# Three small early reads of q and of two weight matrices, added at the start of a fused attention and feed-forward kernel

## The chip, the cores and the metric

The kernel runs on one core of a Trainium2 chip. The metric is device time in microseconds (us) per execution. Executions agree within some tenths of a per cent (the six of the kernel before ran from 325.63 to 327.38 us). A ratio quoted below is the mean time of one kernel's fast runs over the mean of the other kernel's fast runs of the same rounds, so it is not quite the ratio of the medians that stand beside it. Some executions are slow, with a much lower mean granted clock; they are left out of every comparison of times.

Words used: TensorE is PE in the profile (PEld is its weight load), VectorE is DVE, ScalarE is ACT, GpSimd is POOL, SyncE is SP. On the page of the kernel before, the transfers issued by SP and ACT stand on hardware queues (q1 with 41.23 MB and q10 with 0.13 MB), those issued by GpSimd on its software queue (q0 with 11.80 MB). All times inside a profile count from the first instruction.

## The reference

```python
# q, k, v: (8, 8, 576, 64) float32
r = np.maximum(x, 0.0); phi(x) = concat([r * cos_w, r * sin_w], -1)   # cos, sin of pi/2 * pos / S
kv  = einsum('bhsf,bhsd->bhfd', phi(k), v);  z = sum(phi(k), axis=2)
att = einsum('bhsf,bhfd->bhsd', phi(q), kv) / (einsum('bhsf,bhf->bhs', phi(q), z) + 1e-6)
x   = att.transpose(0, 2, 1, 3).reshape(4608, 512)
out = (gelu(x @ w_gate) * (x @ w_val)) @ w_out                        # d_ff 1536
```

## The kernel before

The kernel treats a batch of q, k, v at a time. The three weight matrices are loaded once, cast to bf16 on the way. The first 20 us are a hand-placed start; after them TensorE works without a break in this profile.

```python
    consts = ctx.enter_context(tc.tile_pool(name="consts", bufs=1))     # pools lie one after another
    weights = ctx.enter_context(tc.tile_pool(name="weights", bufs=1))
    inp = ctx.enter_context(tc.tile_pool(name="inp", bufs=2))           # staging of k, q, v in float32
    ...
    load(nc.sync, "k", 0, 0, 2)              # 576 KB each, rows of 2,304 bytes
    load(nc.sync, "k", 0, 2, 4)
    load(nc.sync, "q", 0, 0, NP, 0, JA)      # 512 KB, rows of 1,024 bytes
    load(nc.sync, "v", 0, 0, 2)
    load(nc.sync, "v", 0, 2, 4)
    load(nc.sync, "q", 0, 0, NP, JA, R)      # 640 KB, rows of 1,280 bytes
    ...
        nc.gpsimd.memset(t[:, :, :, D:D + 1], 1.0)      # the two vx tiles
        vx_tiles.append(t)
    gate = consts.tile([128, 1], FP32)
    gate2 = consts.tile([128, 1], FP32)
    ...
    cast_v(0, 0, 2, dve_copy)
    nc.gpsimd.tensor_copy(gate, staged["v", 0][:, 0, 0:1])   # GpSimd waits for v's first half
    load_w(0, 2)                                             # first W group: w_gate, then w_val
    load_w(2, 2)
    nc.gpsimd.tensor_copy(gate2, wg_sb[:, 0, 0:1])           # waits for w_gate's first group
    load_w(4, 2)
    nc.gpsimd.tensor_copy(gate2, wv_sb[:, 0, 0:1])           # waits for w_val's first group
    ...
    dummies(22)                              # products of zeros, to keep TensorE busy at the start
```

The three `gate` copies hold the weights back until v's first half is there, so that W does not compete with v: in the profile before, the first copy starts at 9.39 us and the first W issue at 10.11. They are also good markers in a profile: there each starts when the tile it reads has landed (9.39, 14.29 and 16.57 us, each after a wait for a DMA).

Of the kernel before, what the change touches and what calls it, by code (L numbers as in the profile page):

```python
# [9 lines left out]
FP32 = mybir.dt.float32  # L10
# [6 lines left out]
def kernel(  # L17
# [13 lines left out]
    nc = tc.nc  # L31
# [17 lines left out]
    consts = ctx.enter_context(tc.tile_pool(name="consts", bufs=1))  # L49
# [21 lines left out]
    def rows(t, b):  # L71
        return t[b].rearrange("(m i) (p j) d -> (i p) m (j d)", i=2, j=R)
# [15 lines left out]
    wg_r = moe_w_gate.rearrange("(ct p) j -> p ct j", p=128)  # L88
    wv_r = moe_w_val.rearrange("(ct p) j -> p ct j", p=128)
# [41 lines left out]
    for i in range(2):  # L131
        t = consts.tile([128, NP, R, D + 1], BF16, name=f"vx{i}")
        nc.gpsimd.memset(t[:, :, :, D:D + 1], 1.0)
        vx_tiles.append(t)
    gate = consts.tile([128, 1], FP32)
    gate2 = consts.tile([128, 1], FP32)

# [470 lines left out]
    for n in range(1, NB):  # L608
# [4 lines left out]
        for jt in range(JT):  # L613
# [18 lines left out]
            if b < B:  # L632
# [12 lines left out]
                i = jt - t_nm - 1  # L645
# [8 lines left out]
                i = jt - 1 - n if n <= 2 else -1  # L654
                if 0 <= i < 3:
                    prep_third("k", b, i)
                i = 2 * (jt - 5) if n == 1 else jt - (4 if n == 2 else 0)
# [4 lines left out]
                i = jt - 9  # L662
# [73 lines left out]
```

## Time and profile before

The time before was 327.24 us (median of three runs, 326.32 to 327.38). The profile is of one more run, of 325.91 us.

| what | value | view |
|---|---|---|
| TensorE busy, whole span | 316.8 of 323.9 us | the page, busy times |
| TensorE busy, 20 us to 320 us | all of it | table of stretches |
| v's second half seen landed (its cast starts) | 10.76 us | chain of waits, timeline |
| w_gate's and w_val's first groups seen landed | 14.29 and 16.57 us | timeline, the gate copies |
| first 512-column product | 21.11 us | timeline |

The table of stretches of the kernel before. Columns: the stretch and its length, busy time and number of instructions of each engine, the granted TensorE clock as a share of full speed, the busy share of the DMA engines, GB/s.

```profile
15.00:20.00 5.00, 4.76 (x84) 4.11 (x82) 4.12 (x12) 3.66 (x8) 4.08 (x8) 1.00 1.36 173
20.00:25.00 5.00, 5.00 (x42) 2.88 (x40) 1.70 (x4) 2.86 (x7) 3.65 (x5) 1.00 1.42 192
60.00:320.00 260.00, 260.00 (x1870) 130.70 (x1867) 130.32 (x306) 116.81 (x242) 0.00 (x0) 1.00 0.54 139
```

TensorE is full from 20 us on. A change at the start can gain or lose only by the moment at which this unbroken work begins.

The chain of waits of the kernel before, first 30 us. Columns: start, length, what.

```profile
2.27 0.51 SPq L80
2.78 0.04 issue
2.82 7.92 DMA vf<-in_v_dram
10.74 0.02 issue
10.76 0.86 DVE vx L179
...
13.95 1.29 DVE x_sb L322 x2
...
16.64 0.89 PE ps L372 x16
...
19.49 1.79 PE ps L372 x32
21.27 6.91 PE ps L400 x32
```

The start waits for v's second half and then for VectorE's steps. No weight stands in the chain. The waits of TensorE in the same stretch (who waited for whom: us in total, times, longest) say the same: nothing here is a transfer.

```profile
PE ps L140 <- POOL dummy L113: 1.5, 1, 1.5
PE ps L204 <- ACT qp L160: 1.0, 2, 0.9
PE ps L218 <- DVE vx L179: 0.2, 1, 0.2
PE ps L357 <- DVE x_sb L295: 0.2, 1, 0.2
PE ps L218 <- POOL gate L458: 0.2, 1, 0.2
```

The timeline of the kernel before around the first weights (start, length, engine, line, operation, tiles; in brackets the idle time before it and what ended it):

```profile
14.29 0.18 POOL L461 CAST gate<-wg_sb 128x1 f32<-128x1 bf16 x1 [0.89 <-DMA wg_sb<-in_moe_w_gate_dram]
...
16.48 0.61 PE L372 MATMUL ps<-xT,wg_sb 128*128 128x128 bf16 x8
...
16.57 0.18 POOL L463 CAST gate<-wv_sb 128x1 f32<-128x1 bf16 x1 [0.66 <-DMA wv_sb<-in_moe_w_val_dram]
...
16.93 0.61 PE L372 MATMUL ps<-xT,wv_sb 128*128 128x128 bf16 x8
```

w_val's group lands 0.36 us before its first product starts.

The trace also records every packet of every transfer: start, queue, size and time taken. A 1,024-byte packet of q takes 46 ns, but a few packets at 5.5 to 5.9 us took 380 to 453 ns, soon after q's load begins (its first packet starts at 5.16 us); three at 12.15 us, soon after W begins (at 11.77 us, with 59 ns), took 376 to 414 ns. (W stands for the weights w_gate and w_val.)

### The profile page before, as it was taken

The page shows a single profiled execution, that of the slowest core. Times are in us where ns is not written, and L with a number is a line of the kernel's source. Part 1 is how long each engine was busy: PE and PEld are TensorE (multiplying, and loading weights), DVE is VectorE, ACT ScalarE, POOL GpSimd, SP SyncE. Part 2 cuts the span into 40 slices and gives each one's busy share as a digit, 9 for nine tenths or more (in the row PEclk, how much of TensorE's full clock was granted, in tenths as well). Part 3 has the DMA queues.
Part 4 walks back from the last instruction along what each step waited for, and adds up shares of the span by engine and source line. Part 5 has one row for each costly group of instructions (what it writes and reads, how often), then busy time and mean ns, then how long its engine had stood idle before and what let it go on. Part 6 is the DMA issues. An engine that isn't in the chain of part 4 may idle for free.

```text
span 323.9 us, 6340 instructions
## 1 busy us (share of the span) xinstructions
PE 316.8 (98%) x2451; PEld 164.5 (51%) x2451; DVE 170.3 (53%) x407; ACT 159.3 (49%) x336; POOL 26.0 (8%) x43
## 2 busy tenths in 40 slices
PE   8899999999999999999999999999999999999995
PEld 3574556555754564545544554445544444444443
DVE  5854677759665952793586348544532222222211
ACT  7864858946466832673457336633222332222220
POOL 6684410000000000000000000000000000000000
PEclk9999999999999999999999999999999999999999
DMA  7999999842999689938957990543431111111124
GB/s 274 249 186 273 297 352 366 230 111 51 323 216 354 166 147 383 201 83 251 330 96 157 383 232 1 137 102 78 85 73 33 34 32 32 35 32 32 34 65 98
DMA packets 69102, 53.57 MB, mean 165 GB/s; under 512 B 45392, under 2 KB 54352, under 8 KB 69072
## 3 DMA queue, kind: packets, MB, share of 16 engines
q1 hardware_dynamic: 59264, 41.23, 48.1%
q0 software_dynamic: 9648, 11.80, 15.7%
q8 instruction: 19, 0.31, 0.4%
q10 hardware_dynamic: 160, 0.13, 0.1%
q14 instruction: 11, 0.09, 0.1%
HBM read 37.75 MB, written 9.44 MB: 146 GB/s over the span
## 4 chain that ended last, share of the span: by engine, by line
PE 93%; DMA 2%; DVE 2%; SPq 1%; issue 0%; DVEq 0%
PE ps L400 57%; PE ps L430 28%; PE ps L282 3%; PE ps L241 3%; DMA vf<-in_v_dram 2%; PE ps L204 1%; PE ps L372 1%; PE ps L697 1%; SPq L80 1%; PE ps L357 0%; DVE qp L162 0%; DVE x_sb L322 0%; DVE vx L179 0%; DVE x_sb L295 0%; DVE qT L486 0%
## 5 line engine op out<-in xcount | busy, mean ns | idle before, releaser
L409 DVE TENSOR_TENSOR hT<-gel,ps 128x512 bf16<-128x512 f32 (+1 forms) x114 | 74.1, 650 | 128.9 <-PE ps L400 126.0
L408 ACT ACTIVATE gel<-ps 128x512 f32<-128x512 f32 (+1 forms) x114 | 64.8, 569 | 109.7 <-PE ps L400 108.0
L400 PE MATMUL ps<-xT,wv_sb 128*128 128x512 bf16 (+1 forms) x456 | 110.2, 364 | 0.0
L400 PE MATMUL ps<-xT,wg_sb 128*128 128x512 bf16 (+1 forms) x456 | 110.2, 364 | 0.0
L430 PE MATMUL ps<-wo_sb,hT 128*128 128x512 bf16 x420 | 105.8, 379 | 0.0
L400 PEld LDWEIGHTS <-wv_sb 128*128 128x128 bf16 x456 | 44.6, 98 | 47.0
L400 PEld LDWEIGHTS <-wg_sb 128*128 128x128 bf16 x456 | 44.0, 98 | 46.1
L430 PEld LDWEIGHTS <-hT 128*128 128x128 bf16 x420 | 38.3, 98 | 39.4
L439 ACT COPY o_sb<-ps 128x512 f32<-128x512 f32 x34 | 19.9, 587 | 29.9 <-PE ps L430 27.6
L160 ACT ACTIVATE qp<-qf,sin_t 128x256 bf16<-128x256 f32 x72 | 32.0, 501 | 0.4 <-DMA qf<-in_q_dram 0.4
L160 ACT ACTIVATE kp<-kf,sin_t 128x256 bf16<-128x256 f32 (+1 forms) x73 | 29.9, 479 | 0.9 <-DMA kf<-in_k_dram 0.9
L295 DVE TENSOR_TENSOR x_sb<-ps,rec 128x512 bf16<-128x512 f32 x38 | 26.3, 691 | 1.3
L162 DVE TENSOR_SCALAR qp<-qf,cos_t 128x256 bf16<-128x256 f32 x71 | 21.8, 353 | 2.3 <-DMA qf<-in_q_dram 2.3
L282 PEld LDWEIGHTS <-qT 128*128 128x128 bf16 x304 | 14.6, 98 | 7.9 <-ACT qT L486 0.3
L162 DVE TENSOR_SCALAR kp<-kf,cos_t 128x256 bf16<-128x256 f32 x63 | 18.3, 349 | 0.0
L282 PE MATMUL ps<-kv_sb,qT 128*128 128x65 bf16 x304 | 16.0, 194 | 0.0
L179 DVE CAST vx<-vf 128x1152 bf16<-128x1152 f32 (+1 forms) x15 | 12.0, 804 | 0.8 <-DMA vf<-in_v_dram 0.8
L250 ACT CAST kv_sb<-ps 128x260 bf16<-128x260 f32 x14 | 4.6, 383 | 12.9 <-PE ps L241 12.9
L241 PEld LDWEIGHTS <-kp 64*128 64x128 bf16 x504 | 8.5, 95 | 3.0 <-issue 3.0
L140 PE MATMUL ps<-dummy 128*128 128x512 bf16 x27 | 8.4, 457 | 1.5 <-POOL dummy L113 1.5
L241 PE MATMUL ps<-vx,kp 64*128 64x65 bf16 x504 | 9.3, 191 | 0.0
L294 DVE RECIPROCAL rec<-den 128x8 f32<-128x8 f32 x38 | 7.7, 203 | 1.3
(60 smaller groups left out, 100.6 us busy)
## 6 DMA issues: line engine op xcount, KB each, us to landing
out_dram<-o_sb SPq DMA_DIRECT2D x70, 128.0 KB, 2.6
kf<-in_k_dram SPq DMA_DIRECT2D x12, 576.0 KB, 6.2
vf<-in_v_dram SPq DMA_DIRECT2D x12, 576.0 KB, 8.3
qf<-in_q_dram SPq DMA_DIRECT2D x10, 576.0 KB, 5.0
qf<-in_q_dram POOLq DMA_DIRECT2D x4, 576.0 KB, 12.2
kf<-in_k_dram POOLq DMA_DIRECT2D x4, 576.0 KB, 12.5
vf<-in_v_dram POOLq DMA_DIRECT2D x4, 576.0 KB, 12.8
wg_sb<-in_moe_w_gate_dram POOLq DMA_DIRECT2D x6, 256.0 KB, 6.4
```

Source lines behind the costliest of these rows:

```text
L140: nc.tensor.matmul(bank(to), lhsT=dummy[:, 0:128], rhs=dummy, start=True, stop=True)
L160: nc.scalar.activation(o, i, AF.Relu, scale=tab[:, j:j + 1])
L162: (eng or nc.vector).tensor_scalar(o, i, 0.0, tab[:, j:j + 1], op0=ALU.max, op1=ALU.mult)
L179: copy(vx_tiles[b % 2][:, m0:m1, j0:j1, 0:D], staged["v", b][:, m0:m1, j0 * D:j1 * D].rearrange("p m (j d) -> p m j d", d=D),)
L241: nc.tensor.matmul(bank(6 + i)[:, m * (D + 1):(m + 1) * (D + 1)], lhsT=kp[rr, m, j, :], rhs=vx[rr, m, j, :], start=(j == 0), stop=(j == R ...
L282: nc.tensor.matmul(bank(b0 + h // 4)[:, (h % 4) * (D + 1):(h % 4 + 1) * (D + 1)], lhsT=q_cols(b, t, h), rhs=kv_sb[b][:, h // 2, h % 2, :], ...
L295: nc.vector.tensor_tensor(x, nm[:, :, :, 0:D], rec[:, :, :, None].to_broadcast([128, 2, 4, D]), op=ALU.mult,)
L400: nc.tensor.matmul(bank(b0 + g)[:, 0:w], lhsT=wt[:, ct, js], rhs=xt[:, ct, c0:c0 + w], start=(ct == 0), stop=(ct == CT - 1),)
L408: nc.scalar.activation(gel[:, 0:w], bank(b0)[:, 0:w], AF.Gelu)
L409: nc.vector.tensor_mul(hT[n][:, jt, c0:c0 + w], gel[:, 0:w], bank(b0 + 1)[:, 0:w])
L430: nc.tensor.matmul(bank(to), lhsT=hT[n][:, jt, tt * 128:(tt + 1) * 128], rhs=wo_sb[:, jt, :], start=(jt == 0), stop=(jt == JT - 1),)
L439: copy(o_sb, bank(to))
```

## The change

The intent is to read one word of every region that q's load and the first W groups will read, early, so that whatever a first read costs is paid before the load needs it.

```diff
         nc.gpsimd.memset(t[:, :, :, D:D + 1], 1.0)
         vx_tiles.append(t)
+
+    touch = consts.tile([16, 3, 4], FP32)
+    for i, src in enumerate((rows(q, 0)[:, :, 0:1], wg_r[:, :, 0:1], wv_r[:, :, 0:1])):
+        nc.gpsimd.dma_start(out=touch[:, i, :, None], in_=src[0:128:8])
     gate = consts.tile([128, 1], FP32)
     gate2 = consts.tile([128, 1], FP32)
```

Each of the three transfers reads 16 rows by 4 words. Every later line number is 4 higher in the changed kernel: line 400 there is line 404.

## The prediction

> **What bounds the kernel now.** TensorE. The table of stretches shows PE busy 5.00 of every 5 us from 20 us to the end, and the waits list gives PE only five waits, 3.1 us in all, none on a transfer. So only the first 21 us can yield time. There the chain of waits runs: four load issues on SP to 2.8 us; 7.92 us of v's second half landing (10.74); the DVE steps after it; then PE from 19.1 us on, unbroken. W is not on it: wg's first group is seen landed at 14.29 and wv's at 16.57 (the two GpSimd gate copies in the timeline); their first matmuls start at 16.48 and 16.93.
>
> The transfers are at their limit from 2.75 us to 11 us (360 to 430 GB/s in quarter-microsecond stretches), so v lands when k, q's first part and v (2.9 MB) have gone through. A packet of q's 1,024 B rows takes 46 ns, but the packet records hold three at 5.5 to 5.9 us of 436, 453 and 380 ns: the first reads of q. The same is seen at W's first reads (12.15 us: 414, 395, 376 ns against 60 ns) and at k's (up to 606 ns against 93). The change aims at these stalls.
>
> **What it adds.** Nothing is removed; the other engines keep their order. GpSimd issues three more transfers after the two vx memsets (end 2.36 us). By the twelve W issues (0.95 us the first, 0.75 the usual one) they take about 2.4 us, to 4.8. GpSimd idles 2.26 us there, waiting for k until 4.62, so its kp work starts about 0.2 us late; PE needs its result only at 10.2. No cost. The first W issue took 1.64 us from its start to its first packet[...]. So q's touch reads at about 4.0 us, over 1 us ahead of q's load at 5.1. The words are 3 x 64, twelve per engine if spread over 16[...]. I estimate 0 to 0.2 us of delay to k.
>
> **Gain.** If the touch takes the stall in their place, each stalled engine gets back 0.35 to 0.4 us. [...] I estimate v 0 to 0.4 us earlier, 0.25 in the middle. DVE idled 0.63 us before that cast, so all of it passes into the chain. W's first packets get about 0.35 us back and the first issue perhaps 0.2 (hidden). Net about 0.3 us of 327.
>
> **Predicted: 326.9 us, range 326.0 to 327.7.** Faster by over 2%: 0.01; within 2%: 0.98; slower: 0.01.
>
> **Right if:** no packet of q's load at about 5.5 us and of W's at about 12 us is above 200 ns; the slow ones sit among the 4 B packets on the GpSimd queue at about 4 us; v's second landing and the start of unbroken PE work are each 0.1 to 0.4 us earlier; everything after shifts in parallel.
>
> **Wrong if:** stalls belong to each engine or queue, or to addresses between those touched, so they stay; the tiny packets hold up k by over 0.3 us; another DVE or ACT step swallows the earlier v; or the run spread (1.06 us) hides it.

The 0 to 0.2 us of delay to k is the author's guess, from 3 x 64 words and without a time for them, and the 0 to 0.4 us for v is an estimate from the slow packets alone (380 to 453 ns in place of 46). What the trace has is 16 landings of v's second half, from 9.75 to 10.74 us, and its cast at 10.76, after the last. "At their limit" is the busy share of the DMA engines, 0.91 to 1.13 in every quarter of a microsecond from 2.75 to 11 us. That the slow packets are "first reads" is the forecast's assumption: the very first packets of q and W took 46 and 59 ns in the kernel before.

## The result and the profile after

The changed kernel took 327.68 us (median of 6 runs, 326.95 to 328.11), beside 326.40 us (median of 6 runs, 325.63 to 327.38) for the kernel before. The ratio is 1.0032, 95% interval 1.0010 to 1.0054: within 2%, and a small loss that is clear of the noise. The forecast's range held the median at its upper edge (327.68 against 327.7), but it had expected a gain of 0.3 us where there was a loss of about 1 us. That the range held was luck: the repeat below has a median of 327.82, outside it.

The timeline of the kernel after, GpSimd's touches, and the first weights:

```profile
2.08 0.68 POOL L138 DMA_DIRECT2D touch<-in_q_dram  x1
2.75 0.53 POOL L138 DMA_DIRECT2D touch<-in_moe_w_gate_dram  x1
3.26 0.52 POOL L138 DMA_DIRECT2D touch<-in_moe_w_val_dram  x1
...
10.83 0.76 DVE L183 CAST vx<-vf 128x1152 bf16<-128x1152 f32 x1 [0.75 <-DMA vf<-in_v_dram]
...
14.40 0.18 POOL L465 CAST gate<-wg_sb 128x1 f32<-128x1 bf16 x1 [1.03 <-DMA wg_sb<-in_moe_w_gate_dram]
...
17.52 0.62 PE L376 MATMUL ps<-xT,wv_sb 128*128 128x128 bf16 x8 [0.68 <-DMA wv_sb<-in_moe_w_val_dram]
17.59 0.18 POOL L467 CAST gate<-wv_sb 128x1 f32<-128x1 bf16 x1 [1.56 <-DMA wv_sb<-in_moe_w_val_dram]
```

In this execution w_val's group landed 1.0 us later than in the profile before, and now TensorE waits for it; v's second half was seen landed at almost the same time (10.83 against 10.76 us). The chain of waits of the kernel after changes accordingly:

```profile
2.27 7.02 DMA vf<-in_v_dram
9.29 0.05 issue
9.34 0.77 POOL gate L462
10.11 0.77 POOL wg_sb L94
10.89 0.00 issue
10.89 6.58 DMA wv_sb<-in_moe_w_val_dram
...
20.08 1.79 PE ps L376 x32
21.87 6.91 PE ps L404 x32
```

The unbroken work begins 0.60 us later (21.87 against 21.27). What follows is alike: from the first 512-column product to the end it takes 302.8 us before and 303.1 after.

The stretches in which W streams, first of the kernel before, then of the kernel after (columns as above):

```profile
13.00:15.00 2.00, 1.90 (x27) 1.08 (x23) 1.93 (x6) 2.00 (x5) 1.11 (x3) 1.00 1.44 192
15.00:17.00 2.00, 1.94 (x33) 1.47 (x31) 1.93 (x7) 1.74 (x4) 1.09 (x3) 1.00 1.33 163
```

```profile
13.00:15.00 2.00, 1.90 (x26) 1.05 (x22) 1.93 (x6) 2.00 (x5) 0.97 (x3) 1.00 1.07 140
15.00:17.00 2.00, 1.83 (x31) 1.38 (x28) 1.91 (x7) 1.74 (x4) 1.03 (x2) 1.00 1.09 129
```

The last two columns tell it: W moved at 140 and 129 GB/s instead of 192 and 163. As the experiments show, this is partly a difference between executions, not between kernels, so one profile each is not enough to name a cause.

Two steps of the forecast can be judged at once from the packet records. The touches' 96 packets on GpSimd's queue ran from 5.88 to 8.11 us, not at 4.0; q's load had begun at 4.92. None of these packets took over 22 ns, so the slow ones did not sit among them. And the slow packets of the loads were still there: from 5 to 7 us, the stretch of q's load, four above 250 ns before, four after; from 11 to 13 us, where W begins, nine after, three before.

### The profile page after: what moved, and what is told of

Same layout as the page of the kernel before. It is cut to its first block, busy times and chain, and to the rows that moved or that the text cites. A ratio compares the mean times of both kernels' runs of the same rounds, so it can differ in the third digit from the quotient of the medians.

```text
span 324.8 us, 6343 instructions
## 1 busy us (share of the span) xinstructions
PE 316.9 (98%) x2451; PEld 164.5 (51%) x2451; DVE 170.2 (52%) x407; ACT 159.3 (49%) x336; POOL 27.4 (8%) x46
## 4 chain that ended last, share of the span: by engine, by line
PE 93%; DMA 4%; POOL 0%; DVE 0%; SPq 0%; issue 0%; DVEq 0%
PE ps L404 56%; PE ps L434 28%; PE ps L286 3%; PE ps L245 3%; DMA vf<-in_v_dram 2%; DMA wv_sb<-in_moe_w_val_dram 2%; PE ps L701 1%; PE ps L376 1%; PE ps L208 1%; PE ps L361 0%; SPq L80 0%; POOL wg_sb L94 0%; POOL gate L462 0%; DVE x_sb L299 0%; DVE o_sb L708 0%
```

## The experiments

Four theories stood against each other:

- Address: early reads of q and W change how those loads run.
- Traffic (the first expectations call it "queue"): any tiny packets ahead on a queue take turns on DMA engines that are already full (busy share 0.91 to 1.13 from 2.75 to 11 us in the kernel before; that the packets take turns is the theory, no trace names the engine of a packet).
- Chance: the two kernels are alike, and the start varies from execution to execution.
- Layout: the touch tile is a new tile, and it moves all tiles behind it.

One sum of packet times is used below. The "excess" of a stretch is the time by which the core's packets on SP's queue took longer than 93 ns per 2,304 bytes, added over all packets that start in the stretch, of all 16 engines together. It has a floor: the usual q packets of 1,024 and 1,280 bytes take 46 and 55 ns where this measure allows 41 and 52, so they alone make about 2.2 us of a full stretch from 5 to 7 us and 1.7 us from 9 to 12. The expectations that ask for an excess under 1.5 us could therefore not have been met, whatever the touches did. For the stretch from 5 to 7 us the text adds the excess over the usual 46, 55 and 93 ns: in the two profiles of the kernel before it is 2.4 and 1.1 us. Landing marks are read from the timeline.

### The kernel before and the kernel after, each once more

Edit: none.

> The kernel before, unchanged, as a floor for the noise and for a second profile of the same code. All theories: ratio 1.000 within 0.0015. Theory 'chance' (W's stream has a slow spell in some executions of any kernel): its second profile may show wv's first group landing anywhere from 16.5 to 17.5 us. Theories 'queue' and 'address': it lands again before 16.9 us and PE does not wait for it.

> The changed kernel, unchanged, for a second profile. 'chance': ratio about 1.000 to 1.001. 'queue' and 'address': ratio about 1.003 again, and PE waits 0.4 to 1 us for wv's first group, W's packets again running at only 95 to 155 per half microsecond between 13 and 17 us.

The kernel before gave a ratio of 1.0012 (0.9986 to 1.0038) against itself: with some six runs a side, a tenth of a per cent means nothing. The changed kernel gave 1.0045 (1.0024 to 1.0066; median 327.82 us). The loss is real and repeats. "Chance" falls as an explanation of the whole.

But the marks vary. In the second profile of the kernel before, w_val's group was seen landed at 17.26 us, without any change in the code, as "chance" had allowed; its first product started at 17.18, so the slack was used up, but the waits of TensorE list none for it. In the second profile of the changed kernel TensorE did not wait for w_val either, so that part of the expectation missed; v's second half was cast only at 11.33 us, and something new appeared. The stretches of the second profile of the changed kernel, columns as above:

```profile
8.00:10.00 2.00, 0.84 (x9) 0.49 (x8) 1.44 (x6) 2.00 (x7) 0.15 (x1) 1.00 1.03 380
10.00:12.00 2.00, 1.40 (x45) 1.12 (x45) 1.25 (x2) 0.93 (x3) 2.00 (x3) 0.93 0.89 305
12.00:14.00 2.00, 1.89 (x44) 1.55 (x44) 1.59 (x7) 1.19 (x5) 1.87 (x3) 0.50 1.13 140
14.00:16.00 2.00, 1.78 (x24) 1.31 (x22) 1.33 (x5) 1.50 (x5) 1.36 (x3) 0.72 1.27 132
```

and of the first profile of the kernel before:

```profile
8.00:10.00 2.00, 0.96 (x9) 0.49 (x8) 1.85 (x6) 2.00 (x7) 0.60 (x1) 1.00 1.03 398
10.00:12.00 2.00, 1.66 (x66) 1.49 (x67) 1.37 (x4) 1.37 (x4) 2.00 (x4) 1.00 0.79 283
12.00:14.00 2.00, 1.95 (x53) 1.47 (x46) 1.93 (x8) 1.61 (x6) 1.41 (x2) 1.00 1.24 162
```

The third number from the right is the granted clock. It fell to one half for 3.41 us, from 11.71 to 15.12 us, towards the end of two stretches of 2 us in which TensorE was busy for 0.84 and 1.40 us. The full clock before it lasted 6.83 us, twice as long as the dip. Four of the thirteen fast profiles have the dip (this one, and those of the touches on ScalarE without padding, of 64 bytes of padding and of 256). In those four the clock record first shows the full clock between 4.40 and 4.97 us; in eight of the other nine at 5.11 us or later, and in the last, the first profile of the changed kernel, at 4.72. If one counts stretches of the dip's length, 3.41 us, on from that moment (a choice; no run shows that the clock is set by such stretches), TensorE was busy for 32 to 55% of the stretch just before the dip in the four; in the other nine the emptiest stretch before the unbroken work had 61% or more. So in these thirteen profiles the dip goes with a TensorE that is idle for much of one stretch while v is awaited; that the idleness is its cause was not tested by itself. Such a run can be told by its mean clock of 0.996 or less (0.994 or 0.995 in the four profiles, 0.998 or more in the nine). Counting all fast runs with a known clock: 7 of 38 with the addresses of the kernel before and no touch, 6 of 12 with the changed kernel. Within the kernel before (34 runs), those with a dip took 327.07 us on average and those without 326.52: a dip goes with about 0.6 us.

### Touches of memory that is read anyway

```diff
-    for i, src in enumerate((rows(q, 0)[:, :, 0:1], wg_r[:, :, 0:1], wv_r[:, :, 0:1])):
+    for i, src in enumerate((rows(k, 0)[:, :, 0:1],) * 3):
```

> The three tiny GpSimd transfers stay, but all three read words of k that the first load reads anyway, so nothing of q or W is touched. 'queue' (any three transfers of 4-byte words ahead on the GpSimd queue make W's stream slower): ratio about 1.003, PE waits for wv. 'address' (it is the early reads of q and W that do it): ratio about 1.000. 'chance': about 1.000.

Median 327.09 us, ratio 1.0023 (0.9998 to 1.0047). The middle lies between the two expectations, 1.003 and 1.000, and the interval holds both, so this run alone settles nothing. It showed TensorE waiting 0.7 us for w_val with nothing of W touched, so that wait needs no touch of W.

### The same touches early, on ScalarE's queue

```diff
+    touch = consts.tile([16, 3, 4], FP32)
+    for i, src in enumerate((rows(q, 0)[:, :, 0:1], wg_r[:, :, 0:1], wv_r[:, :, 0:1])):
+        nc.scalar.dma_start(out=touch[:, i, :, None], in_=src[0:128:8])
     load(nc.sync, "k", 0, 0, 2)
```

> The same three touches, issued on ScalarE's queue at its very beginning, so nothing is added to GpSimd's queue and the reads come before q's load. 'queue': no loss; the stalls at q's and W's first packets fall away and the ratio is 0.998 to 1.000. 'address': ratio about 1.003 as with the GpSimd touches. The forecast's own first step (a touch takes the stall in the load's place) says that no packet of q's load and of W's first group is above 200 ns here.

Median 327.36 us, ratio 1.0023 (1.0001 to 1.0046). The interval leaves out the "no loss" of "queue". Here q's reads really came first. The timeline of this kernel, and the summary of its touches:

```profile
0.74 0.45 ACTq L102 DMA_DIRECT2D touch<-in_q_dram  x1
1.22 0.44 ACTq L102 DMA_DIRECT2D touch<-in_moe_w_gate_dram  x1
1.69 0.45 ACTq L102 DMA_DIRECT2D touch<-in_moe_w_val_dram  x1
```

```profile
DMA to landing us min/median/max: 2.5/3.7/4.7
```

A third of the touches' 240 packets, as many as belong to q's touch, had started by 2.89 us, and the last at 5.82; q's load began at 5.10 us and W's at 12.49. No packet of the touches took over 9 ns. Still the excess of the stretch from 5 to 7 us was 5.7 us (4.6 and 3.4 us in the two profiles of the kernel before; over the usual times 3.9 against 2.4 and 1.1), with six packets above 250 ns, the longest 685 ns. From 11 to 13 us W had nine above 250 ns (three and three before). Touching these words early does not take the stall from the load, and the first step of the forecast falls.

### q's load from memory that has just been read; and a touch of every row

```diff
+    srcs["q"] = k
     load(nc.sync, "q", 0, 0, NP, 0, JA)
+    srcs["q"] = q
```

> Wrong result on purpose: the first part of q's load reads the same rows of k, which the two loads ahead of it have just read; no touch. 'First read' (the slow packets at 5.0 to 7.0 us come from memory not read before): the time above the usual one, summed over the packets of that stretch, which was 3.4 to 4.6 us in the two profiles of the kernel before, falls under 1.5 us, and no packet takes over 250 ns. 'Not first reads' (they come from the change to 1,024-byte rows or from what else runs then): it stays between 3 and 5 us. Time: ratio 0.998 to 1.000 in the first case, 1.000 in the second.

The result was wrong. Median 326.34 us, ratio 0.9999 (0.9967 to 1.0032). The excess of 5 to 7 us was 3.5 us, against 3.4 and 4.6 us with the real q (over the usual times 1.2 against 1.1 and 2.4). One packet was above 250 ns (295 ns); the kernel before had two and four, the longest 460 ns. So about half of the slowness at q's start, or more, is there without a first read. Whether the two or three longest packets are, one profile cannot say.

```diff
+    touch = consts.tile([128, 4], FP32)
+    nc.scalar.dma_start(out=touch[:, :, None], in_=rows(q, 0)[:, :, 0:1])
     load(nc.sync, "k", 0, 0, 2)
```

> One touch of q alone, on ScalarE's queue at its beginning, of one word in each of the 128 x 4 rows that q's load will read[...]. 'First read, engine by engine or row by row': no packet of q's load over 250 ns, excess time in 5.0 to 7.0 us under 1.5 us. 'Not first reads': excess 3 to 5 us as before. 'Traffic' for the time: 512 words against 192 in the earlier touch on this queue, so v later than there and a ratio of 1.003 to 1.008.

Median 327.08 us, ratio 1.0017 (0.9989 to 1.0044). Excess 4.6 us (over the usual times 2.3), one packet above 250 ns (361 ns). A touch of every row does not remove it either. "Traffic" missed: the ratio is below 1.003, and v's second cast started at 11.17 us, earlier than the 11.62 of the smaller touch on this queue. This tile takes 16 bytes, 32 with rounding, and moves the others by 32, so its time is not a pure measure of traffic.

### Four times the words; and the touches put last

```diff
-    touch = consts.tile([16, 3, 4], FP32)
-    for i, src in enumerate((rows(q, 0)[:, :, 0:1], wg_r[:, :, 0:1], wv_r[:, :, 0:1])):
-        nc.gpsimd.dma_start(out=touch[:, i, :, None], in_=src[0:128:8])
+    touch = consts.tile([64, 3, 4], FP32)
+    for i, src in enumerate((rows(k, 0)[:, :, 0:1],) * 3):
+        nc.gpsimd.dma_start(out=touch[:, i, :, None], in_=src[0:128:2])
```

> Three tiny GpSimd transfers in the same place, four times the words each (64 rows by 4 words of k, instead of 16 by 4). 'Traffic' (every tiny packet takes a turn on engines that are already full, so k, q and v come later): v's second landing is 1.5 us or more later than in the kernel before (10.8 to 11.0 us) and the ratio is 1.006 to 1.012. 'Per transfer' (the cost is in three more transfers, not in their packets): ratio 1.002 to 1.004 as with the small decoys. 'Chance': 1.000 to 1.002.

Median 327.87 us, ratio 1.0037 (1.0008 to 1.0066), which misses the 1.006 to 1.012 of "traffic" in its middle. Its profile fell into the slow state (span 414.8 us, clock 0.755), so no times are taken from it. Its records do show that the packets did not grow in number: 48 of 64 bytes in place of 48 of 16, plus 48 of 4 bytes in both. So this run had not multiplied the packets, only their length, and it tells little about a cost per packet. (Its tile is as large as the changed kernel's, so it too moves what follows.)

```diff
     for m in (0, 2):
         load(nc.gpsimd, "v", 2, m, m + 2)
+
+    touch = consts.tile([16, 3, 4], FP32)
+    for i, src in enumerate((rows(q, 0)[:, :, 0:1], wg_r[:, :, 0:1], wv_r[:, :, 0:1])):
+        nc.gpsimd.dma_start(out=touch[:, i, :, None], in_=src[0:128:8])
```

> The three touches as the last transfers of GpSimd's list, long after all they would help: they can cost only by being there. 'Traffic': ratio 1.000 within 0.002, v and wv land as in the kernel before. 'Chance': the same.

Median 327.11 us, ratio 1.0015 (0.9987 to 1.0042): undecided by time. The touches are issued only behind all of GpSimd's loads, and yet the start was not as in the kernel before: q's 1,280-byte packets, which took 55 ns each in the kernel before, now spread from 55 to 65 ns. (v's second half was cast at 11.57 us, but that mark tells nothing: it varies as much with unmoved tiles, see the table below.) With the same instructions in the same order up to then, only the addresses could differ. The built programs confirm it:

```
first byte in each partition      before    changed   touch last
wg_sb                             27,648     27,712       27,712
kf (first buffer)                 64,512     64,576       64,576
qf (first buffer)                 82,944     83,008       83,008
vf (first buffer)                101,376    101,440      101,440
multiple of 512?                     yes   64 above     64 above
```

The touch tile takes 48 bytes in a partition and 64 with rounding; every pool behind `consts` moves by 64. In the kernel before, all tiles into which q, k, v and W are loaded started on multiples of 512 bytes.

### The addresses alone, and the touches without the addresses

The touches kept, the move undone (64 + 448 = 512 bytes):

```diff
     touch = consts.tile([16, 3, 4], FP32)
     ...
+    pad = consts.tile([128, 112], FP32)
     gate = consts.tile([128, 1], FP32)
```

> The changed kernel with 448 bytes of unused padding after the touch tile, so that the weights and the staging tiles of k, q and v start on multiples of 512 bytes again, as before (the touch tile alone had moved them by 64). The three touches run as in the changed kernel. 'Layout' (the cost is the move of the destinations by 64 bytes): q's 1,280-byte packets at 9.5 to 11.5 us take 55 ns at every percentile from the 10th to the 90th, as in the kernel before (55 to 65 with the move), and the ratio is 1.000 to 1.0015. 'Traffic' (the cost is the tiny packets): the ratio stays at 1.003 to 1.0045. Both at once: ratio about 1.002.

The move alone, in the kernel before (no touch):

```diff
+    pad = consts.tile([128, 16], FP32)
     gate = consts.tile([128, 1], FP32)
```

> The kernel before with 64 bytes of unused padding where the touch tile would stand, and no touch at all: the same instructions, other addresses. 'Layout': ratio 1.002 to 1.004, q's 1,280-byte packets spread from 55 to about 65 ns, v's second landing at 11.3 us or later. 'Traffic': ratio 1.000, packets at 55 ns.

A move by 256 bytes, no touch (`pad` of `[128, 64]`):

> As the last, but with 256 bytes of padding: the destinations stand at 256 modulo 512. If it is the 256-byte boundary that counts [...]: packets at 55 ns throughout and a ratio of 1.000. If the 512-byte boundary counts: as with 64 bytes, 1.002 to 1.004.

The early touches on ScalarE, with the padding of 448 bytes:

> The touches on ScalarE's queue at its beginning, with the padding that keeps the destinations on multiples of 512 bytes: the best case for the change's purpose. If a touch helped at all where its side effect is removed, the ratio is 0.998 to 0.9995 and q's excess packet time in 5 to 7 us is under 1.5 us. If the touches do nothing but take room: ratio 1.000 to 1.002 and 3 to 5 us of excess.

The packets of q's second part (1,280 bytes, starting from 9.5 to 11.5 us; ns at the 10th, 50th and 90th percentile, mean) and the excess from 9 to 12 us, worked out from the packet records of the fast profiles. The excess and the last two columns are in us: the start of v's second cast and of the first 512-column product, from the timelines, with a note where the clock had a dip or TensorE waited 0.7 us for w_val:

```
kernel                            move  touches           10 / 50 / 90   mean   excess 9-12   v cast   512 col.
before                               0  none              55 / 55 / 55   55.0        1.7       10.76      21.11
before again                         0  none              55 / 55 / 55   55.0        1.7       10.96      21.38
q reads k                            0  none              55 / 55 / 55   55.0        1.7       11.28      21.58
touches, 448 bytes of padding      512  GpSimd, early     55 / 55 / 55   55.1        1.8       11.50      22.05
ScalarE touches, 448 of padding    512  ACT, early        55 / 55 / 55   55.0        1.7       11.47      21.77
256 bytes of padding               256  none              55 / 55 / 55   55.0        1.6       11.61      22.77  dip
64 bytes of padding                 64  none              55 / 59 / 66   59.5        4.5       10.94      21.93  dip
changed                             64  GpSimd, early     55 / 56 / 65   58.4        4.0       10.83      21.71  wait
changed again                       64  GpSimd, early     55 / 59 / 67   59.1        4.6       11.33      22.36  dip
touches last                        64  none early        55 / 59 / 65   59.0        4.1       11.57      21.75
touches of k                        64  GpSimd, early     55 / 55 / 65   57.7        3.7       11.66      22.81  wait
ScalarE touches                     64  ACT, early        55 / 55 / 65   57.8        3.5       11.62      22.57  dip
touch of every row                  32  ACT, early        55 / 58 / 65   59.1        5.0       11.17      21.32
```

The line between the two groups is the address of the destinations: on a multiple of 256 bytes (moves of 0, 256 and 512) or off it (moves of 32 and 64); touches or none, early or late, on either queue make no difference to it. A move by 128 was not run, so these runs do not tell a boundary of 256 bytes from one of 128. A move by 256 bytes did no harm to these packets (55 ns at all three percentiles). (Its time, 1.0010, does not tell it from the other moves: its profile and two of its six runs have the dip of the clock.) The sources in memory are the same and the destinations moved: the mean of a 1,280-byte packet is 5 to 8% longer at 32 or 64 above a multiple (57.7 to 59.5 ns against 55.0), and not longer at 256. But not every packet into a moved tile was slower: q's 1,024-byte packets took 46 ns at the 10th, 50th and 90th percentile in all seven moved kernels but the touch of every row (54 at the 90th), and W's 512-byte packets, from 13 to 21 us, 60 ns at all three in both groups. Why an address off the multiple costs some packets time and others none was not shown. Later packets show the two groups again: from 20 to 60 us the 4,608-byte packets on GpSimd's queue took 178 ns at all three on multiples of 256, and 194 at the 90th off them.

The times:

| kernel | median us | ratio (95% interval) |
|---|---|---|
| touches, 448 bytes of padding | 326.91 | 1.0006 (0.9989 to 1.0023) |
| ScalarE touches, 448 bytes of padding | 326.59 | 1.0001 (0.9982 to 1.0020) |
| 64 bytes of padding, no touch | 326.98 | 1.0013 (0.9996 to 1.0029) |
| 256 bytes of padding, no touch | 327.08 | 1.0010 (0.9991 to 1.0030) |

With the addresses put back, the touches cost nothing that can be measured, and bring nothing: on ScalarE's queue, in the best case for the intent, 1.0001, with an excess of 5.4 us at q's start where under 1.5 was hoped for. (That excess could not have fallen so low; over the usual times it is 3.5 us, against 2.4 and 1.1 in the kernel before.) The move alone gives a middle of 1.0013, below the expected 1.002, with an interval that just includes 1, and v's second cast started at 10.94 us, not at 11.3 or later. Put together over all rounds (fast runs; two standard errors; the chips of the rounds were not all the same), with the 34 comparison runs of the kernel before at a mean of 326.57 us (the six of its own repeat, mean 326.85, are left out):

```
the changed kernel, 12 runs                           327.76   +1.2 +- 0.4
move of 64, no early touch (two kernels), 10 runs     327.05   +0.5 +- 0.3
touches, addresses put back (two kernels), 12 runs    326.76   +0.2 +- 0.3
move of 256, no touch, 6 runs                         326.98   +0.4 +- 0.6
move of 64, touches of k, 6 runs                      327.20   +0.6 +- 0.7
move of 64, ScalarE touches, 6 runs                   327.22   +0.7 +- 0.5
```

So the kernels with the move and no early touch are slower by about 0.5 us. The difference between the changed kernel and the same touches with the addresses put back (GpSimd, six runs, mean 326.84) is 0.9 +- 0.5 us (they were timed in different rounds): most of the loss goes when the addresses are put back. That the move and the touches together cost more than their sum of 0.7 us is not shown: the uncertainties cover it.

That the slower packets carry this loss is not shown either, and three things speak against it as the only cause. From 9 to 12 us they add 2 to 3 us of excess, summed over 16 engines, so 0.1 to 0.2 us per engine (an estimate from the table). The move by 256 bytes, whose packets are not slower, has a middle of +0.4 us, though with a wide error. And v's second cast starts no earlier with unmoved packets: 11.26 us on average in the six profiles on multiples of 256, 11.30 in the seven off them. What does set the start is seen in the last columns. In the seven profiles without a mark, of both groups, the first 512-column product follows v's second cast by 10.15 to 10.55 us; in the six with a dip of the clock or a wait of 0.7 us for w_val, by 10.88 to 11.16. One profile of six has such a mark on multiples of 256, and five of seven off them. Whether the move makes them likelier, or they fell so by chance, thirteen profiles cannot say.

## Why the prediction was right or wrong

The number was right in the sense that its range held the result and that it stood by "within 2%". Its sign was wrong, and the reasons that gave the sign were wrong.

- TensorE bounds the kernel, and "only the first 21 us can yield time": right. From the first 512-column product to the end, the profiles of the kernels before and after took 302.8 to 303.1 us.
- "If the touch takes the stall in their place, each stalled engine gets back 0.35 to 0.4 us": wrong; this is the step that failed. On GpSimd's queue the touches ran at 5.9 to 8.1 us, behind the start of q's load. On ScalarE's queue q's ran before it, and the excess at q's start was 5.7 us without padding and 5.4 with it, no lower than in the kernel before (4.6 and 3.4). Nor did the touches take a stall themselves: none of their packets took over 22 ns. The forecast had taken packets that are slow at the start of q's and W's loads for packets that are slow because they read first. A load of q from rows of k that had just been read had an excess of 3.5 us. That the stalls might stay was among the forecast's own ways to be wrong. (Its "360 to 430 GB/s" also passed over the slow place itself: from 5.50 to 6.00 us the table of stretches has 295 and 311.)
- "q's touch reads at about 4.0 us": wrong by 1.9 us. It took 3.8 us from the start of its issue to the first packet, where the first W issue had taken 1.66 (the forecast has 1.64); from the end of the issue it is 3.1 us against 0.70. Why is not settled.
- "They take about 2.4 us, to 4.8 … kp starts about 0.2 us late": the three issues took 1.73 us and ended at 3.78, and GpSimd still waited 0.58 us for k. There was no delay, and no cost, as the forecast concluded.
- "Nothing is removed; the other engines keep their order", taken as all that the change does: this is the omission. The order was kept, the addresses were not. A tile of 48 bytes moved the weights and the staging tiles off their 256-byte boundaries, and q's 1,280-byte packets were slower in every kernel here whose tiles stood off such a boundary (57.7 to 59.5 ns on average) and in no other (55.0 to 55.1). A term for the addresses was missing from the sum: the kernels with the move and no early touch were 0.5 +- 0.3 us slower, though by which path is not shown.
- "0 to 0.2 us of delay to k": not contradicted. With the addresses put back the touches cost 0.2 +- 0.3 us in all.
- "All of it passes into the chain", so that TensorE's start follows v: right as a mechanism (10.15 to 10.55 us behind v's second cast in seven profiles), with two additions that the forecast did not have: w_val's slack of 0.36 us was gone in the first profile after (a wait of 0.7 us), and in four of the thirteen profiles the start has 3.41 us at half clock, which goes with about 0.6 us of time. v itself was not earlier: 10.83 us in the profile after, 10.76 before.

Left open: what makes some packets slow soon after q's and W's loads begin; how the whole loss of 1.2 us divides, and by which path the move costs time; and whether the dip of the clock, 6 of 12 runs against 7 of 38, is really more frequent in the changed kernel or was drawn so. No version beat the kernel before.

## What to carry to other kernels

Here a new tile of 48 bytes in an early pool moved every tile behind it by 64 bytes: compare the addresses of the two built programs before you explain a small loss by what the new instructions do, and try a padding to a multiple of 256 bytes when a transfer's destination has moved off one (q's 1,280-byte packets took 55.0 to 55.1 ns on average at moves of 0, 256 and 512, 57.7 to 59.5 at 32 and 64). Slow packets at the start of a load are not yet a cost of first reads (with q read from rows of k that had just been read, 1.2 us over the usual times stayed, against 1.1 and 2.4); point the load at memory that has just been read and see whether they stay, before you build a remedy. Work out what a measure shows when nothing is wrong before you set a limit on it: here the limit of 1.5 us lay below its floor. And where the difference is a few tenths of a per cent, take several profiles of each kernel: here one landing varied by 0.7 us between two profiles of the same code.
